# Query, key and value products of eight tiles in three wide steps, with scratch ordered by query, key and value

## The chip, the cores and the metric

The kernel runs on one core of a Trainium2 chip. The metric is device time in microseconds (us) for one execution. The core has five engines with an instruction stream each: PE (TensorE, matrix multiplication; its weight loads are listed apart as PEld), DVE (VectorE), ACT (ScalarE), POOL (GpSimd) and SP (SyncE, which here issues all DMA transfers).

## The reference

One transformer block on 2048 rows of 512 numbers: a normalisation without scale or shift, attention over a dilated local window, a residual, another normalisation, a squared-ReLU MLP and a second residual.

```python
S, D, H, Dh, W, dil, F = 2048, 512, 32, 16, 8, 2, 1792

def layernorm(x): return (x - mean(x)) / sqrt(var(x) + 1e-5)

def attention(x):
    q, k, v = split(x @ wqkv)              # each S x 512: 32 heads of 16
    # row s looks at rows s, s-2, s-4, ... s-14; rows below 0 are masked
    logits = q[s] . k[s - 2*w] * Dh**-0.5  # w = 0..7, per head
    o = softmax(logits over w) @ v[s - 2*w]
    return o @ wo

h   = x + attention(layernorm(x))
r   = maximum(layernorm(h) @ w1 + b1, 0)
out = h + (r * r) @ w2 + b2
```

## The kernel before

**Tiles and steps.** The 2048 rows are cut into 16 tiles of 128 rows, numbered t = 0 to 15. A tile is not 128 neighbouring rows: partition p of a tile holds every eighth row, `i = t % 4` and the parity `e` of the row being fixed in a tile, so that the rows of a window (two apart) lie in the same parity `e`. The attention and the MLP work in eight steps s = 0 to 7 of two tiles (`RI = 2`); four tiles (`R = 4`) with the same half of the rows and the same parity form a unit.

**Matrix products.** Every product is done in three passes of reduced-width operands: each factor is split in a high part (a cast, `hi`) and a low part (the difference, `lo`). `mm3` issues the twelve matmuls of one product over four blocks of the inner dimension: four of high by high, four of low activations by high weights, four of high activations by low weights. The casts run on ScalarE; the differences on VectorE or GpSimd.

**Slots.** The program order is written out by hand. `now["slot"]` counts slots, one product (or one MLP step) each. A product's neighbours are put down with `at(d, fn)`, to be issued d slots later, and `after(d, fn)`, the same but behind the slot's attention work. `end_slot(pe)` closes a slot: it adds the declared TensorE time `pe` to `now["pe"]`, issues what is due (`run(due)`), then lets `pump` take pieces from the generator `attention()` until the declared VectorE time `now["dve"]` has caught up with `now["pe"]`, then issues the `late` list. `transposes` and some other functions add to these two counters as well. The numbers are declared costs of this planner, not measurements; they only set the order of the instructions.

**Query, key and value (tiles 0 to 15).** For each tile: `load_x`, `x_stats` (statistics on VectorE, the reciprocal root on GpSimd), `x_norm` (ScalarE for t >= 4), `x_T` (four TensorE transposes, with a cast to `xh` on ScalarE and a difference `xl` on VectorE), then four products `qkv(t, gp)`. A product has 384 columns: 128 of the query, 128 of the key and 128 of the value, of two of the eight groups of heads. Its result lies in one of four PSUM banks in turn (`bank()`: `mm`, `mm`, `acc0`, `acc1`). One slot later `evac` copies it on ScalarE into a half of the staging buffer `y2`, beside the result of the other tile of the pair; when both are there, `store` sends this to the scratch `qkv_d` in DRAM, in one transfer. `store_halo` copies, for each of four `gp`, the pad rows that the first window needs, inside the scratch, two slots after the store of tile 0. `stored` notes which (unit, gp) the attention may read.

Slots 0 to 15 are the products of tiles 0 to 3. `first_phase(t0)` then does tiles t0 and t0 + 1 in eight slots, for t0 = 4, 6, 8, 10, 12 and 14 (slots 16 to 63), and prepares tiles t0 + 2 and t0 + 3 meanwhile: `x_stats` in its slots 0 and 1, `x_norm` in 4 and 5, `x_T` in 6 and 7. In its even slots `weight_job` loads a piece of `wo` or `w1` into `raw`; five slots later ScalarE casts it and GpSimd takes the difference. The phases of tiles 12 and 14 also contain the beginning of step 0 behind the attention: `o_T` (transposes of the attention's result `o`, cast to `oh` on ScalarE, difference `ol` on VectorE), `wo_product`, `h_add` (residual and statistics, VectorE), `h_norm` and `h_T`.

**Attention.** The generator `attention()` runs through 32 items (s, gp), each of which covers two tiles and two groups of heads: loads of `k`, `v`, `q` from the scratch, `dots` and its sums on VectorE, the exponential on ScalarE, and `weigh`, a product on VectorE followed by three halving additions on GpSimd, which end in `o`. The first eight items take gp in the outer loop; from step 2 on, all four gp of a step follow each other.

**MLP.** For each step, 14 slots: `mlp1(s, f)` makes 128 columns of the hidden layer (twelve matmuls of 256 columns), `hidden` one slot later activates, squares and casts it on ScalarE and takes the low part `rl` on GpSimd (VectorE in the last step), and `mlp2` adds the block to the output three slots later (`LAG`). Between them stand the next step's `o_T` (slots 3 and 4) and `wo_product` (slots 6 and 7). In the first MLP block the weights `w2` come in as well: `load_w2` into a `raw2`, and `split_w2`.

**Staging rows.** `row()` gives out buffers of 128 x 512 from one pool of `ROWS = 15`; `xt`, `xh`, `xl`, `raw`, `raw2`, `h`, `hn`, `oh`, `ol`, `hh` and `hl` all live there. When all are taken, the next writer waits for the last reader of the oldest. The last low part of `w2`, `w2_l[13]`, lives in a row as well, since the buffer of `y2`, reused for `w2` behind the products, has room for three blocks of 512.

Of the kernel before, what the change touches and what calls it, by code (L numbers as in the profile page):

```python
# [8 lines left out]
F32 = mybir.dt.float32  # L9
F32R = mybir.dt.float32r  # L10
# [4 lines left out]
S, D, H, DH, W, F = 2048, 512, 32, 16, 8, 1792  # L15
P = 128
KB = D // P
FB = F // P
R = 4
RI = 2  # L20
NS = S // P // RI
G = 8
GH = H // G
GC = GH * DH
CH = S // 2
PAD = W
EPS = 1e-5
NEG = -4.0e9
ROWS = 15
LAG = 3  # L30
SLOW = 1.1
DELAY = 3
# [6 lines left out]
def block_kernel(ctx, tc, x, wqkv, wo, w1, b1, w2, b2, out):  # L39
    nc = tc.nc  # L40

    const = ctx.enter_context(tc.tile_pool(name="const", bufs=1))
    wpool = ctx.enter_context(tc.tile_pool(name="wpool", bufs=1))
# [3 lines left out]
    dram = ctx.enter_context(tc.tile_pool(name="dram", bufs=1, space=bass.MemoryType.DRAM))  # L47
# [1 line left out]
    ctx.enter_context(tc.manual_schedule())  # L49

    CS = (CH + PAD) * GC
    qkv_d = dram.tile([2, G // 2, 3, 2, CH + PAD, GC], F32, name="qkv_d")

    def chain(e, g, c, r, ap):
        block = ((e * (G // 2) + g // 2) * 3 + c) * 2 + g % 2
        return bass.AP(tensor=qkv_d.tensor, offset=qkv_d.offset + block * CS + r * GC, ap=ap)


# [12 lines left out]
    wq_h = wpool.tile([P, KB, 3 * D], F32R, name="wq_h", tag="big_h")  # L73
    wq_l = wpool.tile([P, KB, 3 * D], F32R, name="wq_l", tag="big_l")
# [4 lines left out]
    w2_h, w2_l = {}, {}  # L79

    def row(name, shape=(P, D), dt=F32):
        return work.tile(list(shape), dt, name=name, tag="row", bufs=ROWS)

# [7 lines left out]
    def at(delta, fn, *a):  # L91
        due.setdefault(now["slot"] + delta, []).append((fn, a))

    def after(delta, fn, *a):
        late.setdefault(now["slot"] + delta, []).append((fn, a))

    def end_slot(pe):
        now["pe"] += pe
        run(due)
        pump()  # L100
        run(late)
        now["slot"] += 1

    def run(chores):
        todo = chores.get(now["slot"], [])
        while todo:
            fn, a = todo.pop(0)
            fn(*a)
# [43 lines left out]
    def transposes(src):  # L152
        tr = psum.tile([P, KB, P], F32, name="tr", bufs=2)
        for k in range(KB):
            nc.tensor.transpose(tr[:, k, :], src[:, k * P:(k + 1) * P], ident)  # L155
        now["pe"] += 0.45
        return tr
# [14 lines left out]
    def mm3(ps, lh, ll, rh, rl):  # L172

        terms = [(lh, rh, k) for k in range(KB)] + [(ll, rh, k) for k in range(KB)]
        terms += [(lh, rl, k) for k in range(KB)]
        for n, (l, r, k) in enumerate(terms):
            nc.tensor.matmul(ps, l(k), r(k), start=(n == 0), stop=(n == 3 * KB - 1))  # L177
# [4 lines left out]
    stored = set()  # L182
# [160 lines left out]
    def pump(until=None):  # L343

        while (done[until] < G) if until is not None else (now["dve"] < now["pe"]):
            t = next(stream, "end")
            if t == "end":
                now["dve"] = 1e9
                return
            if t is None:  # L350
                now["dve"] = max(now["dve"], now["pe"])
                return
            dve(t * SLOW)


    xt, xT = {}, {}
# [13 lines left out]
    def x_T(t):  # L370
        tr = transposes(xt.pop(t))
        xT[t] = row("xh", (P, KB, P), F32R), row("xl", (P, KB, P), F32R)
        at(0, hi_T, tr, [xT[t][0]])
        after(0, lo_T, tr, [xT[t][0]], [xT[t][1]])

    nbank = [0]

    def bank():
        tag = ("mm", "mm", "acc0", "acc1")[nbank[0] % 4]
        nbank[0] += 1  # L380
        return psum.tile([P, D], F32, name="mm", tag=tag, bufs=2 if tag == "mm" else 1)


    GP = 2 * GC

    def pair(w, k, gp):
        return w[:, k].rearrange("p (c n) -> p c n", c=3)[:, :, gp * GP:(gp + 1) * GP]
# [4 lines left out]
            nc.sync.dma_start(chain(0, g, 2, 0, [[G * 3 * CS, 2], [GC, PAD], [1, GC]]),  # L392
                              chain(0, g, 2, PAD, [[0, 2], [0, PAD], [1, GC]]))

    def store(t, gp, y):
        b, r = divmod(t, 8)
        e, i = divmod(r, 4)
        nc.sync.dma_start(chain(e, 2 * gp, 0, PAD + CH // 2 * b + i,
                                [[R * GC, P], [CS, 6], [1, RI * GC]]), y)
        if t == 0:  # L400
            at(2, store_halo, gp)
        if i == R - RI:
            stored.add((t // R, gp))

    ys = {}
    y2 = wpool.tile([P, 2, 6, RI * GC], F32, name="y2", tag="y2")

    def evac(t, gp, ps):
        if t % RI == 0:
            ys[gp] = y2[:, nbank[0] // RI % 2]  # L410
        y = ys[gp]
        nc.scalar.copy(y[:, :, t % RI * GC:(t % RI + 1) * GC],  # L412
                       ps[:, :3 * GP].rearrange("p (j c) -> p j c", j=6))
        if t % RI == RI - 1:
            at(0, store, t - t % RI, gp, ys.pop(gp))

    def qkv(t, gp):

        ps = bank()
        xh, xl = xT[t]  # L420
        mm3(ps[:, :3 * GP], lambda k: xh[:, k, :], lambda k: xl[:, k, :],
            lambda k: pair(wq_h, k, gp), lambda k: pair(wq_l, k, gp))
        at(1, evac, t, gp, ps)

    raws = {}

# [39 lines left out]
    def o_T(s, j):  # L466
        pump(until=s)
        tr = transposes(o_t[s][:, j, :])
        oT[s, j] = row("oh", (P, KB, P), F32R), row("ol", (P, KB, P), F32R)
        at(0, hi_T, tr, [oT[s, j][0]])  # L470
        after(0, lo_T, tr, [oT[s, j][0]], [oT[s, j][1]])
# [13 lines left out]
    def wo_product(s, j):  # L485
        ps = psum.tile([P, D], F32, name="wo", tag="tr", bufs=2)
        oh, ol = oT.pop((s, j))
        mm3(ps, lambda k: oh[:, k, :], lambda k: ol[:, k, :],
            lambda k: wo_h[:, k, :], lambda k: wo_l[:, k, :])
        at(1, h_add, s, j, ps)  # L490
        after(3, h_norm, s, j)
# [3 lines left out]
    def h_T(s, j):  # L495
        if j == 0:
            hT[s] = ([row("hh", (P, KB // 2, RI, P), F32R) for _ in range(2)],
                     [row("hl", (P, KB // 2, RI, P), F32R) for _ in range(2)])
        hh, hl = hT[s]
        tr = transposes(hn.pop((s, j)))  # L500
        hs_, ls_ = [t[:, :, j] for t in hh], [t[:, :, j] for t in hl]
        due.setdefault(now["slot"], []).insert(0, (hi_T, (tr, hs_)))
        at(0, lo_T, tr, hs_, ls_)
# [87 lines left out]
    for n in range(16):  # L591
        gp, t = divmod(n, 4)
        if n in (1, 2):
            x_T(n + 1)
        qkv(t, gp)
        if n < 6:
            for k in (0, 1):
                at(0, hi_wqkv, n // 2 + 1, n % 2 * 2 + k)
                after(0, lo_wqkv, n // 2 + 1, n % 2 * 2 + k,
                      nc.gpsimd if k else nc.vector)  # L600
        if n == 1:
            load_wqkv(3)
        if n == 13:
            consts()
        if n in (5, 6, 12, 14):
            at(0, load_x, n - 1 if n < 7 else n // 2)
        if n in (8, 9):
            at(0, x_stats, n - 4)
        if n in (12, 13):
            at(0, x_norm, n - 8)  # L610
        if n in (14, 15):
            x_T(n - 10)
        end_slot(1.95)
# [3 lines left out]
    def first_phase(t0):  # L617
        for n in range(8):
            gp, t = n // 2, t0 + n % 2
            if t0 + 3 < 16:  # L620
                if n in (0, 1):
                    at(0, x_stats, t0 + 2 + n)
                if n in (4, 5):
                    at(0, x_norm, t0 - 2 + n)
                if n in (6, 7):
                    x_T(t0 - 4 + n)
            if t0 + 5 < 16 and n in (4, 6):
                at(0, load_x, t0 + 2 + n // 2)
            k = 8 * ((t0 - 12) // 2) + n - 4
            if k in (10, 11):  # L630
                h_T(0, k - 10)
            qkv(t, gp)
            if jobs and n % WJ == 0:
                at(0, weight_job)
            if k in (0, 1):
                at(0, load_h, 0, k)
                o_T(0, k)
            if k in (3, 4):
                wo_product(0, k - 3)
                now["pe"] += 2.6  # L640
            if k in (7, 8, 9):
                at(0, load_w2, k - 7)
            end_slot(1.95)

    def load_w2(f):
        raws[f] = row("raw2")
        nc.sync.dma_start(raws[f], w2[f * P:(f + 1) * P, :])

    for t in range(R, 16, RI):
        first_phase(t)  # L650


    big2_h = wpool.tile([P, 12, D], F32R, name="w2_h", tag="big_h")
    big2_l = wpool.tile([P, 12, D], F32R, name="w2_l", tag="big_l")
    big2_x = wpool.tile([P, 3, D], F32R, name="w2_x", tag="y2")
    for f in range(12):
        w2_h[f], w2_l[f] = big2_h[:, f, :], big2_l[:, f, :]
    w2_h[12], w2_l[12], w2_h[13] = [big2_x[:, n, :] for n in range(3)]
    w2_l[13] = row("w2l", dt=F32R)

    def split_w2(f):
        raw = raws.pop(f)
# [63 lines left out]
```

## Time and profile before

| | us |
|---|---|
| three runs, timed | 535.2, 536.5, 537.06 (median 536.5) |
| the profiled execution, timed | 534.84 |
| its span, from first to last instruction | 533.1 |
| TensorE busy | 520.7 (98%), 3186 matmuls and transposes |
| VectorE busy | 376.1 (71%) |
| GpSimd busy | 317.9 (60%) |
| ScalarE busy | 262.1 (49%) |
| granted TensorE clock, mean | 1.0 |

How to read the lines that follow. A row of a timeline gives the start in the span, the time that the row covers, the engine, the source line, the operation, what it writes <- what it reads, the shapes, how many instructions the row holds, and in brackets the idle time of the engine before it with what released it. SPq is the queue of DMA issues on SP. Matmuls overlap in time, so that the price of one is the distance between two starts, not its duration. In a row of a wait the numbers are the total, the count and the longest. In a row of a stretch stand, after the length, the busy time of PE, PEld, DVE, ACT and POOL with the number of instructions, the granted clock, the share of the DMA engines' time and GB/s. A row of the chain of waits that ended last begins with the time in the span and the length. Line numbers are those of the kernel above.

### The profile page before, as it was taken

The page shows a single profiled execution, that of the slowest core. Times are in us where ns is not written, and L with a number is a line of the kernel's source. Part 1 is how long each engine was busy: PE and PEld are TensorE (multiplying, and loading weights), DVE is VectorE, ACT ScalarE, POOL GpSimd, SP SyncE. Part 2 cuts the span into 40 slices and gives each one's busy share as a digit, 9 for nine tenths or more (in the row PEclk, how much of TensorE's full clock was granted, in tenths as well). Part 3 has the DMA queues.
Part 4 walks back from the last instruction along what each step waited for, and adds up shares of the span by engine and source line. Part 5 has one row for each costly group of instructions (what it writes and reads, how often), then busy time and mean ns, then how long its engine had stood idle before and what let it go on. Part 6 is the DMA issues. An engine that isn't in the chain of part 4 may idle for free.

```text
span 533.1 us, 9022 instructions
## 1 busy us (share of the span) xinstructions
PE 520.7 (98%) x3186; PEld 479.1 (90%) x3186; DVE 376.1 (71%) x569; ACT 262.1 (49%) x607; POOL 317.9 (60%) x435
## 2 busy tenths in 40 slices
PE   6999999999999989999999999999999999999996
PEld 5899999999999868988989898898989889898995
DVE  5569999887897898996998699599869502202111
ACT  4524554455248446545636454563645445254541
POOL 4515499687495398778678677867867852251000
PEclk9999999999999999999999999999999999999999
DMA  8577979687587453633643364364434102001001
GB/s 251 155 233 196 298 234 317 201 269 239 159 252 263 135 157 91 191 116 102 182 142 108 111 190 119 100 183 137 112 106 140 44 0 81 1 0 41 2 0 41
DMA packets 70661, 75.96 MB, mean 143 GB/s; under 512 B 6744, under 2 KB 47704, under 8 KB 70616
## 3 DMA queue, kind: packets, MB, share of 16 engines
q1 hardware_dynamic: 70616, 75.39, 46.7%
q8 instruction: 25, 0.41, 0.3%
q14 instruction: 20, 0.16, 0.1%
HBM read 58.50 MB, written 16.91 MB: 141 GB/s over the span
## 4 chain that ended last, share of the span: by engine, by line
PE 61%; POOL 2%; DVE 0%; ACT 0%; issue 0%; POOLq 0%
PE mm L177 27%; PE acc L530 9%; PE acc L532 9%; PE acc L531 9%; PE wo L177 6%; PE tr L155 2%; POOL pr L292 1%; POOL rl L118 1%; POOL h L483 0%; POOL rs L134 0%; DVE pr L283 0%; POOL rs L132 0%; DVE h L537 0%; ACT hh L115 0%; POOL o L292 0%
## 5 line engine op out<-in xcount | busy, mean ns | idle before, releaser
L292 POOL TENSOR_TENSOR pr<-pr 128x512 f32<-128x512 f32 (+1 forms) x128 | 133.0, 1039 | 47.6 <-DVE pr L283 42.5
L118 POOL TENSOR_TENSOR rl<-r,rh 128x256 fp32r<-128x256 f32 x98 | 72.1, 739 | 82.9 <-ACT rh L115 73.6
L509 ACT ACTIVATE r<-mm,b_sb 128x256 f32<-128x256 f32 x112 | 53.3, 476 | 123.1 <-PE mm L177 112.3
L272 DVE TENSOR_TENSOR pr<-qp,k 128x1024 f32<-128x1024 f32 x64 | 76.0, 1187 | 5.8 <-ACT qp L216 3.5
L283 DVE TENSOR_TENSOR pr<-ex,v 128x1024 f32<-128x1024 f32 x64 | 77.9, 1217 | 2.8
L532 PE MATMUL acc<-w_h,rl 128*128 128x512 f32 x192 | 75.0, 391 | 2.7 <-POOL rl L118 2.7
L530 PE MATMUL acc<-w_h,rh 128*128 128x512 f32 x192 | 76.5, 398 | 0.0
L531 PE MATMUL acc<-w_l,rh 128*128 128x512 f32 x192 | 75.9, 395 | 0.0
L177 PE MATMUL mm<-hh,w_h 128*128 128x256 f32 x448 | 72.5, 284 | 0.0
L177 PEld LDWEIGHTS mm<-hh,w_h 128*128 128x128 f32 x448 | 66.4, 189 | 6.5
L177 PE MATMUL mm<-hl,w_h 128*128 128x256 f32 x448 | 72.0, 283 | 0.0
L177 PE MATMUL mm<-hh,w_l 128*128 128x256 f32 x448 | 72.0, 283 | 0.0
L177 PEld LDWEIGHTS mm<-hl,w_h 128*128 128x128 f32 x448 | 61.8, 192 | 0.0
L177 PEld LDWEIGHTS mm<-hh,w_l 128*128 128x128 f32 x448 | 61.7, 192 | 0.0
L412 ACT COPY y<-mm 128x384 f32<-128x384 f32 x64 | 30.1, 480 | 63.6 <-PE mm L177 40.0
L177 PE MATMUL mm<-wq_h,xh 128*128 128x384 f32 x256 | 56.7, 342 | 0.3 <-ACT wq_h L115 0.3
L177 PE MATMUL mm<-wq_l,xh 128*128 128x384 f32 x256 | 55.3, 335 | 0.2 <-DVE wq_l L118 0.2
L177 PE MATMUL mm<-wq_h,xl 128*128 128x384 f32 x256 | 55.0, 335 | 0.4 <-DVE xl L118 0.4
L118 DVE TENSOR_TENSOR hl<-tr,hh 128x256 fp32r<-128x256 f32 x32 | 12.1, 418 | 56.8 <-ACT hh L115 56.8
L510 ACT ACTIVATE r<-r 128x256 f32<-128x256 f32 x112 | 46.9, 418 | 3.5
L115 ACT CAST rh<-r 128x256 fp32r<-128x256 f32 x112 | 45.6, 407 | 3.6
L532 PEld LDWEIGHTS acc<-w_h,rl 128*128 128x128 f32 x192 | 36.1, 188 | 11.8 <-POOL rl L118 3.6
(78 smaller groups left out, 869.3 us busy)
## 6 DMA issues: line engine op xcount, KB each, us to landing
k<-qkv_d SPq DMA_DIRECT2D x48, 288.0 KB, 2.8
v<-qkv_d SPq DMA_DIRECT2D x48, 288.0 KB, 2.7
qkv_d<-y SPq DMA_DIRECT2D x32, 384.0 KB, 3.9
xt<-in_A_x_dram SPq DMA_DIRECT2D x16, 256.0 KB, 4.2
q<-qkv_d SPq DMA_DIRECT2D x32, 128.0 KB, 2.8
h<-in_A_x_dram SPq DMA_DIRECT2D x16, 256.0 KB, 4.0
out_dram<-h SPq DMA_DIRECT2D x16, 256.0 KB, 3.2
raw<-in_B_w_dram SPq DMA_DIRECT2D x16, 224.0 KB, 4.3
```

Source lines behind the costliest of these rows:

```text
L115: nc.scalar.copy(dst, src)
L118: eng.tensor_tensor(out=dst, in0=src, in1=h, op=ALU.subtract)
L177: nc.tensor.matmul(ps, l(k), r(k), start=(n == 0), stop=(n == 3 * KB - 1))
L272: nc.vector.tensor_tensor(out=pr.rearrange("p i w h d -> p i w (h d)"), in0=qp[:, j].unsqueeze(2).to_broadcast([P, RI, W, GC]), in1=kwin, ...
L283: nc.vector.tensor_tensor(out=p2, in1=vwin, op=ALU.mult, in0=e1[:, :, :, j * GH:(j + 1) * GH].unsqueeze(4).to_broadcast([P, RI, W, GH, DH]))
L292: nc.gpsimd.tensor_tensor(out=dst, in0=p2[:, :, :w], in1=p2[:, :, w:2 * w], op=ALU.add)
L412: nc.scalar.copy(y[:, :, t % RI * GC:(t % RI + 1) * GC], ps[:, :3 * GP].rearrange("p (j c) -> p j c", j=6))
L509: nc.scalar.activation(r, ps, AF.Relu, bias=b1_sb[:, f:f + 1])
L510: nc.scalar.activation(r, r, AF.Square)
L530: nc.tensor.matmul(a, rh[:, js], w2_h[f], start=(f == 0), stop=False)
L531: nc.tensor.matmul(a, rh[:, js], w2_l[f], start=False, stop=False)
L532: nc.tensor.matmul(a, rl[:, js], w2_h[f], start=False, stop=(f == FB - 1))
```

## The change

- Tiles 4 to 11 go through a new `middle_phase(t0)`: six slots for a pair of tiles instead of eight. A slot is one product `qkv_of(t, c)` of 512 columns: all of the query (c = 0), the key (1) or the value (2) of one tile. Tiles 0 to 3 and 12 to 15 keep their products of 384 columns.
- In a middle phase the next pair's `x_stats` stand in slots 0 and 1, `x_norm` in 3 and 4, `x_T` in 4 and 5, `load_x` in 3 and 5, and the weight jobs in 0, 1, 3 and 4. A slot declares 2.65.
- The scratch is ordered by parity, then query/key/value, then the eight groups of heads; before, the pair of groups came ahead of query/key/value. A wide product's result is stored in one transfer of 512 KB for a pair of tiles; a narrow product's result (384 KB) now takes two transfers, one for each group. For tiles 4 to 11 a unit is noted in `stored` only behind the value's store, for all four `gp` at once.
- A half of `y2` grows from six to eight blocks of 64 columns. Its buffer then has room for four blocks of `w2`, so `w2_l[13]` moves there from a row of the pool, and the pool has 14 rows.

```diff
-ROWS = 15
+ROWS = 14
...
-    qkv_d = dram.tile([2, G // 2, 3, 2, CH + PAD, GC], F32, name="qkv_d")
+    qkv_d = dram.tile([2, 3, G, CH + PAD, GC], F32, name="qkv_d")
 
     def chain(e, g, c, r, ap):
-        block = ((e * (G // 2) + g // 2) * 3 + c) * 2 + g % 2
+        block = (e * 3 + c) * G + g
...
-    def store(t, gp, y):
+    def store(t, gp, c, y):
         b, r = divmod(t, 8)
         e, i = divmod(r, 4)
-        nc.sync.dma_start(chain(e, 2 * gp, 0, PAD + CH // 2 * b + i,
-                                [[R * GC, P], [CS, 6], [1, RI * GC]]), y)
+        pos = PAD + CH // 2 * b + i
+        if c is None:
+            for j in range(2):
+                nc.sync.dma_start(chain(e, 2 * gp + j, 0, pos,
+                                        [[R * GC, P], [G * CS, 3], [1, RI * GC]]), y[:, :, j])
+        else:
+            nc.sync.dma_start(chain(e, 0, c, pos, [[R * GC, P], [CS, G], [1, RI * GC]]), y)
         if t == 0:
             at(2, store_halo, gp)
         if i == R - RI:
-            stored.add((t // R, gp))
+            if c is None:
+                stored.add((t // R, gp))
+            elif c == 2:
+                stored.update((t // R, gp) for gp in range(G // 2))
 
     ys = {}
-    y2 = wpool.tile([P, 2, 6, RI * GC], F32, name="y2", tag="y2")
-
-    def evac(t, gp, ps):
+    y2 = wpool.tile([P, 2, G, RI * GC], F32, name="y2", tag="y2")
+
+    def evac(t, gp, c, ps):
+        j = 6 if c is None else G
         if t % RI == 0:
-            ys[gp] = y2[:, nbank[0] // RI % 2]
-        y = ys[gp]
+            ys[gp, c] = y2[:, nbank[0] // RI % 2, :j]
+        y = ys[gp, c]
         nc.scalar.copy(y[:, :, t % RI * GC:(t % RI + 1) * GC],
-                       ps[:, :3 * GP].rearrange("p (j c) -> p j c", j=6))
+                       ps[:, :j * GC].rearrange("p (j c) -> p j c", j=j))
         if t % RI == RI - 1:
-            at(0, store, t - t % RI, gp, ys.pop(gp))
+            if c is None:
+                y = y.rearrange("p (c j) n -> p c j n", c=3)
+            at(0, store, t - t % RI, gp, c, y)
+            del ys[gp, c]
+
+    def qkv_of(t, c):
+
+        ps = bank()
+        xh, xl = xT[t]
+        cs = slice(c * D, (c + 1) * D)
+        mm3(ps, lambda k: xh[:, k, :], lambda k: xl[:, k, :],
+            lambda k: wq_h[:, k, cs], lambda k: wq_l[:, k, cs])
+        at(1, evac, t, 0, c, ps)
...
-        at(1, evac, t, gp, ps)
+        at(1, evac, t, gp, None, ps)
...
+    def middle_phase(t0):
+        for n in range(6):
+            c, t = n // 2, t0 + n % 2
+            if n in (0, 1):
+                at(0, x_stats, t0 + 2 + n)
+            if n in (3, 4):
+                at(0, x_norm, t0 - 1 + n)
+            if n in (4, 5):
+                x_T(t0 - 2 + n)
+            if n in (3, 5):
+                at(0, load_x, t0 + 4 + n // 4)
+            qkv_of(t, c)
+            if n % 3 != 2:
+                at(0, weight_job)
+            end_slot(2.65)
...
     for t in range(R, 16, RI):
-        first_phase(t)
+        middle_phase(t) if t < 12 else first_phase(t)
...
-    big2_x = wpool.tile([P, 3, D], F32R, name="w2_x", tag="y2")
+    big2_x = wpool.tile([P, 4, D], F32R, name="w2_x", tag="y2")
     for f in range(12):
         w2_h[f], w2_l[f] = big2_h[:, f, :], big2_l[:, f, :]
-    w2_h[12], w2_l[12], w2_h[13] = [big2_x[:, n, :] for n in range(3)]
-    w2_l[13] = row("w2l", dt=F32R)
+    w2_h[12], w2_l[12], w2_h[13], w2_l[13] = [big2_x[:, n, :] for n in range(4)]
```

## Prediction

> **What bounds the kernel now.** I read the page first, then the table of waits, then busy time by stretch, and last the timelines of the engines around the two places that the change touches.
>
> ```profile
> span 533.1 us, 9022 instructions
> PE 520.7 (98%) x3186; PEld 479.1 (90%) x3186; DVE 376.1 (71%) x569; ACT 262.1 (49%) x607; POOL 317.9 (60%) x435
> ```
>
> ```profile
> PEclk9999999999999999999999999999999999999999
> ```
>
> ```profile
> PE acc L532 <- POOL rl L118: 2.7, 2, 2.0
> ```
>
> ```profile
> 47.00:117.50 70.50, 70.50 (x419) 69.99 (x418) 65.84 (x97) 34.89 (x76) 53.09 (x73) 1.00 0.84 258
> ...
> 159.10:209.30 50.20, 47.40 (x293) 41.72 (x293) 42.34 (x64) 30.68 (x72) 33.72 (x42) 1.00 0.51 161
> ```
>
> The columns after the length are PE, PEld, DVE, ACT, POOL, the granted clock, the DMA share and GB/s. TensorE is the bound: in the stretch of tiles 4 to 11 (47.0 to 117.5) it never idles, and its clock is full. So whatever is saved in the matmul stream there comes off the end, and whatever makes TensorE wait there is added. The first MLP block (159.1 to 209.3) has the one hole behind it: 50.2 us of which 47.4 are busy, and two waits for GpSimd's `rl` make up 2.7 of the idle time. VectorE is at 93% in the stretch that is changed (65.84 of 70.50), and ScalarE, though half idle, carries the copies out of PSUM, the norms and the casts in one fixed order.
>
> **The products.** Start-to-start intervals are the price of a matmul here, since the durations overlap.
>
> ```profile
> 38.57 0.85 PE L177 MATMUL mm<-wq_h,xl 128*128 128x384 f32 x4
> ...
> 40.65 0.85 PE L177 MATMUL mm<-wq_h,xl 128*128 128x384 f32 x4
> ```
>
> ```profile
> 135.96 1.09 PE L177 MATMUL wo<-wo_h,oh 128*128 128x512 f32 x4
> 136.88 1.09 PE L177 MATMUL wo<-wo_h,ol 128*128 128x512 f32 x4
> ```
>
> ```profile
> 269.83 2.72 PE wo L177 x12
> ```
>
> Twelve matmuls of 384 columns take 40.65 - 38.57 = 2.08 us, 173.3 ns each. Twelve of 512 take 2.72 us in the chain, 226.7 ns each. A tile now costs 4 x 2.08 = 8.32 us and will cost 3 x 2.72 = 8.16: the columns are the same 1536, and 12 of 48 matmuls go, with the part of each that isn't columns (173.3 and 226.7 lie on a line of 0.417 ns a column plus 13.3 ns). Eight tiles: 8 x 0.16 = **-1.28 us**, all on the path, since nothing waits there. The other end is the pair of rows at 135.96: in that mixed stretch four matmuls of 512 took 0.92 us, 230 ns each; at 36 x 230 = 8.28 us a tile the gain is 8 x 0.04 = 0.3 us. The slow ones stand right behind narrower products; the middle phases are 512 columns throughout, so I take the chain's value, with 0.04 off (12 x 3.4 ns) at each end of the stretch, where widths change: **-1.2**.
>
> The Trainium skill (TensorE: Matmul & The Clock Gate, Back-to-back issue gap) gives an isolated warm interval of N/2.4 + 2.5 ns. By that the change would bring only 96 x 2.5 ns = 0.24 us; the trace's 173.3 and 226.7 speak against the 2.5.
>
> **The norm that moves closer to its transpose.** Before, `x_norm` runs two slots ahead of `x_T` (n = 4, 5 and 6, 7), two products of 2.08 us. After, it is one slot ahead (n = 3, 4 and 4, 5), one product of 2.72. For most tiles that is enough:
>
> ```profile
> 90.76 0.85 PE L177 MATMUL mm<-wq_h,xh 128*128 128x384 f32 x4
> ```
>
> ```profile
> 91.01 0.48 ACT L412 COPY y<-mm 128x384 f32<-128x384 f32 x1 [1.61 <-PE mm L177]
> 91.39 0.82 ACT L150 ACTIVATE xt<-xt,rs 128x512 f32<-128x512 f32 x1
> ```
>
> The norm of tile 10 ends at 92.21, 1.45 us after a product began at 90.76, and a wide product leaves 2.72. For tile 6 it isn't enough, because there ScalarE is held up.
>
> ```profile
> 47.00 0.95 PE L177 MATMUL mm<-wq_h,xh 128*128 128x384 f32 x4
> ```
>
> ```profile
> 59.81 0.60 PE L155 MATMUL tr<-ident,xt 128*128 128x128 f32 x4
> ```
>
> ```profile
> 52.42 0.86 ACT L412 COPY y<-mm 128x384 f32<-128x384 f32 x2 [3.52 <-DMA qkv_d<-y]
> 57.97 0.86 ACT L412 COPY y<-mm 128x384 f32<-128x384 f32 x2 [4.69 <-PE mm L177]
> 58.71 0.83 ACT L150 ACTIVATE xt<-xt,rs 128x512 f32<-128x512 f32 x1
> ```
>
> ```profile
> 47.91 0.38 SPq L398 DMA_DIRECT2D qkv_d<-y  x1
> 48.34 0.54 SPq L209 DMA_DIRECT2D q<-qkv_d  x1
> 52.34 1.19 SPq L392 DMA_DIRECT2D qkv_d<-qkv_d  x2
> 53.62 0.35 SPq L450 DMA_DIRECT2D raw<-in_A_wo_dram  x1
> 54.07 0.38 SPq L398 DMA_DIRECT2D qkv_d<-y  x1
> ```
>
> ```profile
> DMA to landing us min/median/max: 2.6/3.9/6.5
> ```
>
> Products 16, 17, 18 start at 47.00, 49.1, 51.2 (2.08 apart), so the copy of product 18 could begin about 53.5; yet ScalarE begins it at 57.97 (the row puts the wait down to TensorE, which was long done). It needs the half of `y2` that the store issued at 54.07 reads, and 54.07 + 3.9 is 57.97. That store was late because SP stood from 48.9 to 52.34 before the halo copies, which need the store of 47.91 landed (47.91 + 0.38 + 3.9 = 52.2). Behind the two copies the norm of tile 6 ends at 59.54, and TensorE comes to its transpose at 59.81: 0.27 us to spare.
>
> After, TensorE arrives at that transpose behind four wide products: 47.00 + 4 x 2.72 = 57.88. The norm now stands behind the copy of product 18 alone. With the same landing: 57.97, one copy of 512 columns (0.5, as the next instruction starts 0.48 behind the 512-wide `oh` cast quoted below), the norm 0.83, and 0.2 that I allow to TensorE: 59.5, so TensorE waits 1.6 us. On top come the stores of tiles 0 to 3, issued in two pieces: one issue of 0.38 us more for each, and one to four of these delays arrive here, +0.4 to +1.5. Against that, a piece of half the size may land at the fastest 2.6 instead of 3.9, -1.3. So the wait lies between 0.3 and 3.1; I take **+2.1**, nearer the middle of the row's own landing time than its minimum. What hides this afterwards: nothing, as TensorE has no slack before 190. Tile 7 follows with the same copies already done, and tiles 8 to 11 I price at nothing, by the rows of tile 10.
>
> The Trainium skill (Perfetto Trace Analysis, DMA Optimizations) says that splitting transfers may let the whole end sooner if the DMA engines are mostly idle; the share is 0.84 here, so I don't count on it.
>
> Behind the waiting store on SP stand the next loads of k, v, q, x and the weights, and for those VectorE waits; TensorE waits for no attention before the output products, so half a microsecond there costs nothing. The stores of tiles 4 to 11 become 12 of 512 KB instead of 16 of 384, with three slots of 2.72 between uses of a buffer half instead of three of 2.08: relief, worth nothing at the end. The copies, 6 wide for 8 narrow, hide on ScalarE (34.89 busy of 70.50). That tiles 4 to 7 are all stored only behind their third product costs nothing: by the planner's own clock their last store goes out near 67, and the first item that reads them begins at 103.
>
> **One staging row less.** In program order 15 rows are live or asked for at two places. When the second transposed output of step 0 is cast (slot 5 of the phase of tile 12): 2 `h`, 2 + 2 `oh`/`ol`, 4 `xh`/`xl`, 2 `xt`, 3 `raw`. With 14, `ol` waits for GpSimd to finish with a `raw`.
>
> ```profile
> 131.78 0.69 DVE L118 TENSOR_TENSOR ol<-tr,oh 128x512 fp32r<-128x512 f32 x1 [0.56 <-issue]
> ```
>
> ```profile
> 139.29 0.68 DVE L118 TENSOR_TENSOR xl<-tr,xh 128x512 fp32r<-128x512 f32 x1
> ```
>
> ```profile
> 143.59 0.87 PE L177 MATMUL mm<-wq_h,xh 128*128 128x384 f32 x4
> ```
>
> ```profile
> 133.91 1.16 POOL L118 TENSOR_TENSOR w_l<-raw,w_h 128x448 fp32r<-128x448 f32 x1
> ```
>
> VectorE would stand from 131.8 to 135.1. Behind it `xl` of tile 15 moves from 139.97 to 143.3; TensorE asks for it behind four matmuls of the product at 143.59, at 144.3. 1 us is left: price 0, up to 1 if that cover is gone.
>
> The second place is slot 4 of the first MLP block: 4 `h`, 4 `hh`/`hl`, 2 `oh`/`ol`, 4 `raw2` are 14, and two more are asked for. The trace shows what the 16th does:
>
> ```profile
> 174.82 0.69 DVE L118 TENSOR_TENSOR ol<-tr,oh 128x512 fp32r<-128x512 f32 x1 [3.78 <-PE wo L177]
> ```
>
> ```profile
> 173.64 1.07 PE L177 MATMUL wo<-wo_h,ol 128*128 128x512 f32 x4
> ...
> 175.45 0.64 PE L177 MATMUL mm<-hh,w_h 128*128 128x256 f32 x4
> ```
>
> ```profile
> 170.00 0.59 ACT L115 CAST oh<-tr 128x512 fp32r<-128x512 f32 x1 [1.51 <-DVE w_l L118]
> 170.48 0.62 ACT L115 CAST w_h<-raw 128x512 fp32r<-128x512 f32 x1
> 171.00 0.48 ACT L509 ACTIVATE r<-mm,b_sb 128x256 f32<-128x256 f32 x1
> ```
>
> It waits 3.78 us for the output product that frees a row. With 14, `oh` waits for the same product as well; `oh` is ScalarE's, which has `hidden` of block 4 behind it, and the next product but one needs that PSUM bank. The four readings of `ol` start at 173.64, 0.227 apart, so the last has ended near 174.8. From `oh` to the end of that activation ScalarE takes 1.48 us in the rows (170.00 to 171.48), so the bank is free at 176.3 to 176.4, while TensorE wants it at 175.45: **+0.9**, from 0 (the free row comes from elsewhere) to 2.
>
> **The planner.** A pair of tiles declares 6 x 2.65 + 0.9 = 16.8 instead of 8 x 1.95 + 0.9 = 16.5, so four pairs declare 1.2 more. Adding the declared costs slot by slot, the same attention work (139.31) is out when the MLP begins, against 139.3 now and 138.1 before; from there each `weigh` falls one slot earlier: item 10's second from slot 5 to 4, item 11's from 7 and 9 to 6 and 8.
>
> ```profile
> 186.76 2.44 POOL L292 TENSOR_TENSOR pr<-pr 128x512 f32<-128x512 f32 x2 [4.82 <-DVE pr L283]
> ```
>
> GpSimd idled 4.82 us before this group of item 11, and was late with the `rl` behind it. Weighing one slot earlier puts the group ahead of `h_add`, its statistics and a weight's low part on VectorE, which the planner declares at 0.62 + 0.93 + 0.62 us, and takes away the shorter of the two waits, 2.7 - 2.0; but the two following groups, 2.44 us each and a last addition, now stand ahead of an `rl` that they stood behind. I take **-0.6** of the 2.7, between -2.7 and +3.
>
> **Sum:** -1.2 + 2.1 + 0.9 - 0.6 = +1.2 us. The profiled execution took 534.84 us (span 533.1), 1.66 under the median of 536.5; it becomes 536.0, and the median 537.7. A measurement of this kernel tells about 0.3%, 1.6 us, from no change, so this lies within it, on the slow side.
>
> **The rivals.** *The waits don't come* (0.25): the half stores land near the 2.6 us, tile 6 costs 0.3, and GpSimd, started sooner, loses its 2.7 us of lateness. -1.2 + 0.3 - 2.0 + 0.5 = -2.4: 534.1. For it: 4.82 us of idle GpSimd to fill. Against it: the landing of 3.9 that fits both rows.
>
> *GpSimd's new order* (0.2), the slow side: in the first MLP block two groups of 2.44 us and a little pass ahead of an `rl` that TensorE needs within three slots. It decides if VectorE delivers item 11's second weighing later than two slots (5.6 us) after its place; then each group is waited for nearly in full and 2.7 becomes some 5.2. Without my -0.6 the sum is +1.8, and 2.5 more make +4.3 at worst; at half of that delay it is about +3: 539.5. For it: VectorE is busy for 42.34 of 50.20 us in this stretch, most of its idle time lies before the group (3.78 at 174.82). Against: the group before it leaves earlier.
>
> *The wide products run at 230 ns* (0.05): gain 0.3 instead of 1.2, +2.1: 538.6. By the 2.5 ns of the Trainium skill (TensorE: Matmul & The Clock Gate, Back-to-back issue gap) the time would come out near there too.
>
> That the products stay as many can't be: the counts are in the code.
>
> **The numbers.** The forecast has 0.5: 0.3 of it within 1.6 us, 0.2 above, as its bounds run from about -1 to +3. Faster: 0.22 from the first rival. Same: 0.3 + 0.03 + 0.02 = 0.35. Slower: 0.2 + 0.2 + 0.03 = 0.43. The range goes from the first rival, 534.0, to near the worst of the second, 540.5; the forecast's own is 535.5 to 539.5.
>
> **What would show it.** 36 matmuls a tile 227 ns apart; the transpose of tile 6 waiting 1 to 3 us for ScalarE's norm, with a copy of `y` before it that waits for a store; `oh` of the first MLP block on ScalarE waiting for the output product; an idle of TensorE near 1 us behind that product, and 2 us for `rl`. A gapless stretch of tiles 4 to 11 would prove me wrong by 2 us, and no wait for `rl` by as much again.

## The result, and the profile after

The changed kernel takes 538.35 us (median of 8 runs, 538.0 to 539.0), the kernel before 536.38 (8 runs, 534.8 to 537.06): 1.0047 times as long, with a 95% interval of 1.0035 to 1.0059, so slower by 0.5%. The page of the changed kernel begins:

```profile
span 536.3 us, 8832 instructions
PE 521.2 (97%) x3090; PEld 467.3 (87%) x3090; DVE 382.4 (71%) x569; ACT 261.4 (49%) x599; POOL 317.1 (59%) x435
```

The 96 matmuls are gone and the span is 3.2 us longer. Its table of waits, of TensorE (total, times, longest), says why:

```profile
PE mm L176 <- ACT r L530: 2.0, 2, 1.0
PE acc L553 <- POOL rl L117: 1.6, 2, 0.9
PE wo L176 <- DVE xl L117: 1.6, 1, 1.6
PE tr L154 <- ACT xt L149: 1.3, 1, 1.3
```

Before, the one such entry behind the start was `rl` with 2.7. Three of these four are new. The stretches of tiles 4 to 11 and of the first MLP block, which the prediction showed of before (length, then busy PE, PEld, DVE, ACT, POOL, the granted clock, DMA share, GB/s):

```profile
46.90:117.20 70.30, 69.00 (x321) 56.82 (x319) 66.52 (x98) 33.96 (x67) 51.95 (x73) 1.00 0.85 252
161.10:212.70 51.60, 47.95 (x293) 41.57 (x293) 46.89 (x67) 30.80 (x72) 34.09 (x42) 1.00 0.49 154
```

TensorE now idles 1.3 us in the first, and 3.65 in the second for 2.8 before. To see where the time goes, the program is cut at instructions that every kernel has, and the distance between their starts on TensorE is taken from the traces (us; "wide" kernels have the change's products). From MLP block 1 to TensorE's last matmul all of them take 319.6.

| kernel | `x_T`(5) to first `o_T` | to first output product | to MLP block 0 | to its block 7 | to MLP block 1 |
|---|---|---|---|---|---|
| before | 81.29 | 8.02 | 23.13 | 21.90 | 28.35 |
| before, second profile | 82.59 | 8.02 | 23.13 | 21.90 | 28.35 |
| before, 14 rows | 82.03 | 8.58 | 23.22 | 22.84 | 29.56 |
| before, halo later | 81.06 | 8.04 | 23.13 | 21.91 | 28.42 |
| changed (wide, 14 rows) | 81.56 | 9.82 | 23.19 | 23.13 | 28.50 |
| wide, 14 rows, 2.6 declared | 81.17 | 8.83 | 23.23 | 22.83 | 28.38 |
| wide, 15 rows | 81.48 | 8.36 | 23.26 | 21.91 | 28.25 |
| wide, 15 rows, 2.6 declared | 81.77 | 8.02 | 23.13 | 21.91 | 29.59 |
| wide, 15 rows, halo later | 80.04 | 8.36 | 23.23 | 21.90 | 28.26 |

The first column holds the products and the transpose of tile 6. In the rows with the halo later, where nothing waits, it goes from 81.06 to 80.04: the wide products save 1.02 us. The changed kernel gives back three times that, 1.80 in the second column and 1.23 in the fourth.

**Tile 6, changed kernel** (timelines of ScalarE and TensorE):

```profile
57.99 0.58 ACT L421 COPY y<-mm 128x512 f32<-128x512 f32 x1 [4.38 <-DMA qkv_d<-y]
58.47 0.81 ACT L149 ACTIVATE xt<-xt,rs 128x512 f32<-128x512 f32 x1
59.34 0.65 PE L154 MATMUL tr<-ident,xt 128*128 128x128 f32 x4 [1.30 <-ACT xt L149]
```

The copy starts where the prediction put it, 57.97, now named as waiting for the store, and the transpose stands behind it.

**Ahead of the first output product, changed kernel** (ScalarE, GpSimd, VectorE, TensorE):

```profile
135.04 0.59 ACT L114 CAST xh<-tr 128x512 fp32r<-128x512 f32 x1 [2.76 <-POOL w_l L117]
133.85 1.16 POOL L117 TENSOR_TENSOR w_l<-raw,w_h 128x448 fp32r<-128x448 f32 x1
137.18 0.68 DVE L117 TENSOR_TENSOR xl<-tr,xh 128x512 fp32r<-128x512 f32 x1
137.91 1.18 PE L176 MATMUL wo<-wo_h,oh 128*128 128x512 f32 x4 [1.64 <-DVE xl L117]
```

ScalarE stands until GpSimd's low part frees a row at 135.0; the cast of tile 14 is late, so is its low part on VectorE, and TensorE doesn't begin the output product, because `wo` and the transposes share two PSUM buffers (the tag `tr`) and the one it wants still holds what `xl` reads.

**First MLP block, changed kernel** (ScalarE, then TensorE):

```profile
176.77 0.59 ACT L114 CAST oh<-tr 128x512 fp32r<-128x512 f32 x1 [6.84 <-PE wo L176]
...
178.07 0.48 ACT L530 ACTIVATE r<-mm,b_sb 128x256 f32<-128x256 f32 x1
...
178.60 0.73 PE L176 MATMUL mm<-hh,w_h 128*128 128x256 f32 x4 [0.97 <-ACT r L530]
```

`oh` stands until an output product gives a row back, the activation `r` stands behind it on ScalarE, and TensorE waits for the PSUM bank that `r` reads.

### The profile page after: what moved, and what is told of

The parts are those of the page before. It is cut to its first block, busy times and chain, and to the rows that moved or that the text cites. A ratio compares the mean times of both kernels' runs of the same rounds, so it can differ in the third digit from the quotient of the medians.

```text
span 536.3 us, 8832 instructions
## 1 busy us (share of the span) xinstructions
PE 521.2 (97%) x3090; PEld 467.3 (87%) x3090; DVE 382.4 (71%) x569; ACT 261.4 (49%) x599; POOL 317.1 (59%) x435
## 4 chain that ended last, share of the span: by engine, by line
PE 60%; POOL 3%; DVE 2%; issue 1%; POOLq 0%; DVEq 0%
PE mm L176 26%; PE acc L551 9%; PE acc L552 9%; PE acc L553 8%; PE wo L176 6%; PE tr L154 2%; POOL pr L291 1%; POOL rl L117 1%; DVE pr L282 0%; POOL h L504 0%; DVE st L125 0%; DVE w_l L117 0%; DVE h L496 0%; DVE lg L319 0%; DVE h L558 0%
## 5 line engine op out<-in xcount | busy, mean ns | idle before, releaser
L421 ACT COPY y<-mm 128x384 f32<-128x384 f32 (+1 forms) x56 | 29.2, 526 | 57.0 <-PE mm L176 33.6
L176 PE MATMUL mm<-wq_h,xh 128*128 128x384 f32 (+1 forms) x224 | 55.6, 370 | 0.0
L176 PE MATMUL mm<-wq_h,xl 128*128 128x384 f32 (+1 forms) x224 | 53.9, 362 | 0.4 <-DVE xl L117 0.4
L176 PE MATMUL mm<-wq_l,xh 128*128 128x384 f32 (+1 forms) x224 | 53.4, 360 | 0.0
L176 PEld LDWEIGHTS mm<-wq_h,xl 128*128 128x128 f32 x224 | 41.3, 190 | 4.7 <-DVE xl L117 0.8
```

Of the source, the lines that this page charges most:

```text
L421: nc.scalar.copy(y[:, :, t % RI * GC:(t % RI + 1) * GC], ps[:, :j * GC].rearrange("p (j c) -> p j c", j=j))
```

## The experiments

Each was run beside the kernel before, in three rounds on three chips; ratios are to the kernel before on the same chip.

### The kernel before, once more

> The kernel before, unchanged, once more: its profile of 534.84 us lies 1.5 under its median of 536.38, so what do its other executions spend? Theory of waits: products and transposes take the same time in every execution, and the spread of 534.8 to 537.06 lies in TensorE's few waits; a longer span than 533.1 shows a longer wait for the transpose of tile 6 (0.27 us to spare before) or for rl in the first MLP block (3.3 us of excess in the first profile, start to start). Rival: the spread is even, each stage a little longer. Time 536.4, within 0.2% of the runs beside it.

536.03 us, ratio 0.9997 (0.9986 to 1.0007). Its profile has 536.12 us, span 534.3, and the 1.2 us more than in the first profile lie in one stage, the first column. Timelines of ScalarE and TensorE in this second profile:

```profile
59.42 0.86 ACT L412 COPY y<-mm 128x384 f32<-128x384 f32 x2 [4.65 <-DMA qkv_d<-y]
60.17 0.82 ACT L150 ACTIVATE xt<-xt,rs 128x512 f32<-128x512 f32 x1
61.05 0.66 PE L155 MATMUL tr<-ident,xt 128*128 128x128 f32 x4 [0.69 <-ACT xt L150]
```

TensorE waits for the norm of tile 6 in the kernel before as well; some 0.4 us more lie at tile 5's `xl`, 50.37. The 0.27 us to spare were those of one execution. What differs is a landing: the store of `y` ahead of the halo copies is issued at 47.91 and 47.89, but SP's wait for it is 3.4 us in the first profile and 4.9 in the second (waits of SP's queue):

```profile
SPq L392 <- DMA qkv_d<-y: 3.4, 1, 3.4
```

```profile
SPq L392 <- DMA qkv_d<-y: 4.9, 1, 4.9
```

### The norm two slots ahead again

> The changed kernel with x_norm of the middle phases one slot earlier (slots 2 and 3, two slots ahead of the transpose as before the change). Theory of waits: the norm of tile 6 then stands ahead of the copy of product 18, TensorE no longer stands 1.35 us at its transpose, and all that follows comes 1.35 us earlier: 537.0. Rival, attention sets the pace: GpSimd's w_l that frees the row at 135.0 depends on VectorE and not on TensorE, so the wait ahead of the first output product grows from 1.8 to 3.1 us and the time stays 538.3.

```diff
-            if n in (3, 4):
-                at(0, x_norm, t0 - 1 + n)
+            if n in (2, 3):
+                at(0, x_norm, t0 + n)
```

538.06 us, ratio 1.0037 (1.0025 to 1.005): 0.3 less than the changed kernel, not 1.35. The wait at tile 6 is gone, and the wait ahead of the output product has not grown, so the rival is wrong as it stood. But its thought came true elsewhere: VectorE, busy 66.52 us of the 70.30 of that stretch in the changed kernel, gives tile 9's `xl` too late for a TensorE that comes earlier (TensorE, this run):

```profile
86.42 1.20 PE L176 MATMUL mm<-wq_h,xl 128*128 128x512 f32 x4 [0.49 <-DVE xl L117]
```

In this profile that takes back 0.65 us start to start, and its first tiles were 0.56 later than the changed kernel's.

### Fifteen rows; and both

> The changed kernel with 15 staging rows again (2 KB won by one buffer instead of two for q and for lg, and by placing zero in an unused part of y2). Theory of waits: ScalarE's xh of tile 14 no longer waits 2.76 us for GpSimd's w_l, and its oh of the first MLP block no longer 6.84 us for the output product; TensorE's waits of 1.8 us ahead of the first output product and of 1.2 us ahead of block 5 of the first MLP block go: 538.35 - 3.0 = 535.3. The wait of 1.35 us at tile 6 stays. Rival, attention sets the pace: TensorE comes 3.0 us earlier to the second half of the first MLP block and waits there so much longer for rl and for ScalarE (3.3 us now, 6 then): 538.

> Both edits together: 15 rows and x_norm two slots ahead. Theory of waits: the terms add, 538.35 - 1.35 - 3.0 = 534.0; what is left against the kernel before is the 1.05 us that the wide products save and the stores in two pieces, so 0.4% faster than before. Rival, attention sets the pace: no faster than the better of the two alone, 535.3 to 537.

```diff
-ROWS = 14
+ROWS = 15
...
-    zero = const.tile([PAD, GC], F32, name="zero")
+    zero = y2[:PAD, 1, 6, :GC]            # behind the allocation of y2
...
-        q = att.tile([P, 2, RI, GC], F32, name="q")
+        q = att.tile([P, 2, RI, GC], F32, name="q", bufs=1)
...
-                lg = att.tile([P, RI, W, 2, GH], F32, name="lg")
+                lg = att.tile([P, RI, W, 2, GH], F32, name="lg", bufs=1)
```

15 rows: 535.1 us (expected 535.3), ratio 0.9977 (0.9967 to 0.9988), faster than the kernel before. In ScalarE's timeline the cast of tile 14 no longer stands, and the fourth column is back at 21.91:

```profile
132.20 0.61 ACT L113 CAST xh<-tr 128x512 fp32r<-128x512 f32 x1
```

The one row costs the changed kernel 538.35 - 535.1 = 3.2 us, 2.7 of them in the two columns (9.82 - 8.36 and 23.13 - 21.91). (The edit makes single buffers of `q` and `lg` as well, so 3.2 is the row less whatever that costs, which no run shows apart.) With the norm early as well: 534.8, ratio 0.9975 (0.9965 to 0.9986). The expected 534.0 was missed: between these two the timed runs show no difference, though the profiles do (533.6 and 532.6 of span). What the early norm is worth is a few tenths here, and I can't say it closer.

### Fourteen rows in the kernel before

> The row part alone in the kernel before: 14 rows, y2 with eight blocks of which the narrow products use six, w2_l[13] in it; products, stores and scratch as before. Theory of rows: the two waits that 14 rows made in the changed kernel need nothing else of the change, so TensorE stands about 1.8 us ahead of the first output product and 1.2 us in the first MLP block: 536.3 + 3.0 = 539.3. Rival, the waits come only where the new order of the attention's pieces puts GpSimd's w_l late: 536.3 to 537.5.

```diff
-ROWS = 15
+ROWS = 14
...
-    y2 = wpool.tile([P, 2, 6, RI * GC], F32, name="y2", tag="y2")
+    y2 = wpool.tile([P, 2, G, RI * GC], F32, name="y2", tag="y2")
```

(`evac` takes the first six blocks; `w2_l[13]` in `y2` as in the change.) 537.27 us against 536.01, ratio 1.003 (1.0017 to 1.0043): +1.3 by the medians and 1.6 by the ratio, half of what was expected. The time is in the rival's range, yet both waits are there without the rest of the change, 0.56 (8.58) and 0.94 (22.84) in place of 1.8 and 1.2: so the rows alone don't explain 3.2.

### The scratch and the stores alone

> The order of the scratch alone in the kernel before, and with it stores in two pieces for all 16 tiles (64 transfers for 32); 15 rows, 384 columns throughout. Theory: the path doesn't see it but at the transpose of tile 6, where the kernel before already waits 0 to 1.3 us in its two profiles, and where the later stores add up to 1: 536.3 to 537.3. Rival, SP's queue: 32 more issues of 0.4 to 0.5 us each hold up the loads for the attention, and so GpSimd and the first MLP block: 538 or more.

```diff
-    qkv_d = dram.tile([2, G // 2, 3, 2, CH + PAD, GC], F32, name="qkv_d")
+    qkv_d = dram.tile([2, 3, G, CH + PAD, GC], F32, name="qkv_d")
...
-        block = ((e * (G // 2) + g // 2) * 3 + c) * 2 + g % 2
+        block = (e * 3 + c) * G + g
...
-        nc.sync.dma_start(chain(e, 2 * gp, 0, PAD + CH // 2 * b + i,
-                                [[R * GC, P], [CS, 6], [1, RI * GC]]), y)
+        y = y.rearrange("p (c j) n -> p c j n", c=3)
+        for j in range(2):
+            nc.sync.dma_start(chain(e, 2 * gp + j, 0, PAD + CH // 2 * b + i,
+                                    [[R * GC, P], [G * CS, 3], [1, RI * GC]]), y[:, :, j])
```

535.5 us against 536.01, ratio 0.9994 (0.9982 to 1.0006): less than the theory's 536.3, and no cost that can be told, although 32 transfers are issued more. More issues on SP's queue as a cost of the change are out; SP standing before the halo copies is another matter, below.

### What a wide slot declares

> The changed kernel with 15 rows and 2.6 declared for a wide slot instead of 2.65, so that a pair of tiles declares 16.5 as before the change and the attention's pieces fall in the first MLP block as they did before. Theory: the shift was worth nothing (block 7 of the first MLP block to the next block's start took 28.36 us before the change and 28.26 with 15 rows): 535.1 within 0.5, with the waits of 0.92 and 2.15 us for rl of the kernel before in place of 1.07, 0.86 and 1.1. Rival, the step of the prediction: the later order was worth 0.6, so 535.7 or more.

> The changed kernel (14 rows) with 2.6 declared for a wide slot, so that the attention's pieces lie as before the change. 14 rows cost 3.2 us in the changed kernel (538.35 against 535.1) but 1.3 in the kernel before (537.27 against 536.0). Theory of order: the difference comes from where the declared 16.8 puts the attention's pieces around tile 14's cast, so with 2.6 the wait ahead of the first output product falls from 1.6 to about 0.5 us, and the cost of 14 rows against the same kernel with 15 (535.77) is 1.3 to 1.6: 537.2. Rival, the wide products themselves make the rows scarce: 3.2 us again, 539.0.

```diff
-            end_slot(2.65)
+            end_slot(2.6)
```

With 15 rows: 535.77 us, ratio 0.9993 (0.9981 to 1.0006), 0.7 more than with 2.65, though the two intervals overlap a little. With 14: 537.56, ratio 1.003 (1.0016 to 1.0044). So with 2.6 the lost row costs 1.8 us, with 2.65 3.2, and the wait ahead of the output product falls from 1.80 to 0.81: the later order of the attention's pieces makes the same missing row dearer. It costs 0.34 there without any row missing (8.36 against 8.02), and in return the timed runs with 15 rows give it 0.7. The profiles' 28.25 against 29.59 overstate this: with 2.6 the slowest of twelve executions was profiled, one in which the granted clock fell.

The clock of each execution is on record. A fall to half for 3.4 us, as the last section shows it, lowers the mean of 534 us by 0.003; the mean tells that a whole fall came, not where. Medians (and numbers) of the executions at 0.997 or less, and of those above:

| kernel | 0.997 or less | above |
|---|---|---|
| before, in the three rounds | 536.48 to 536.54 (61) | 535.27 to 535.54 (32) |
| wide, 15 rows, 2.6 declared | 536.26 (7) | 534.86 (5) |
| wide, 15 rows | 535.53 (1) | 534.96 (11) |
| wide, 14 rows, 2.6 declared | 538.34 (7) | 536.28 (5) |

Where the clock didn't fall, the two declared costs give the same time with 15 rows, 534.86 and 534.96. So by these executions the order of 2.65 shortens nothing by itself; its 0.7 is that the clock falls in one execution of twelve instead of seven. The lost row costs 1.4 there with 2.6 (536.28 - 534.86), and is still dearer with 2.65.

### The addition of b2 moved

> The changed kernel with 15 rows, x_norm two slots ahead, and GpSimd's addition of b2 to h moved 12 slots on (out of the first MLP block, where two of them of 1.75 and 1.29 us stand between rl's). Theory: the waits for rl near the end of that block (0.86 and 1.1 us) go, 534.8 - 2.0 = 532.8; the wait of 1.07 us for ScalarE's activation behind the exponential stays. Rival, GpSimd is late there by the attention's additions, which wait for VectorE, and the moved additions make other rl late: 534.8.

```diff
-        nc.gpsimd.tensor_tensor(out=h, in0=h, in1=b2_sb, op=ALU.add)
+        after(12, lambda: nc.gpsimd.tensor_tensor(out=h, in0=h, in1=b2_sb, op=ALU.add))
```

534.93 us, ratio 0.9984 (0.9975 to 0.9993): no gain over 534.8. I had overlooked step 0: its two additions, 12 slots on, now fall into the same block (GpSimd, 185.84 and 187.82). The waits for `rl` are gone, but ScalarE, whose activation stands behind the exponential in its order, makes TensorE wait instead (ScalarE, then TensorE):

```profile
193.46 0.28 ACT L337 ACTIVATE ex<-lg 128x128 f32<-128x128 f32 x1 [3.67 <-DVE lg L333]
...
194.88 1.01 PE L175 MATMUL mm<-hh,w_h 128*128 128x256 f32 x4 [2.05 <-ACT r L530]
```

### The halo copies later

> The changed kernel with 15 rows, and the halo copies of the last three pairs of groups issued five slots behind the store of tile 0 instead of two; x_norm stays one slot ahead. Theory: the norm of tile 6 is late because SP stands before the halo copies until a store has landed, and the next stores queue behind; with the halo later SP goes on, the copies of y come earlier and the wait at the transpose of tile 6 (1.06 us of excess in the run with 15 rows) goes: 535.1 - 1.0 = 534.1. Rival, the stores land late by themselves, halo or not: 535.1, wait as before.

> 15 rows, x_norm two slots ahead, and the halo copies later. Theory: with the norm early the wait of tile 6 is gone already (534.8), so the halo adds nothing on the path: 534.8. Rival, a freer ScalarE and SP also bring the attention's loads earlier and shorten the waits in the first MLP block (3.3 us): 533.5.

> The kernel before with the halo copies later, nothing else. Theory: its executions spread over 534.4 to 537.8 because the transpose of tile 6 waits 0 to 1.3 us for the same stall of SP; without it the median falls by about 0.8 to 535.4 and the upper end below 537. Rival, the spread comes from the first MLP block, where the granted clock falls to 0.6 for 3 us in some profiles behind the wait of 2.4 us for rl (1.2 us more): median 536.2 and the same spread.

```diff
-            at(2, store_halo, gp)
+            at(2 if gp == 0 else 5, store_halo, gp)
```

Wide products, 15 rows, halo later: 534.1 us as expected (five executions), ratio 0.9964 (0.9951 to 0.9977), the lowest median here; the interval overlaps that of 15 rows alone. SP goes on, the stores behind follow, and the norm ends 1 us before TensorE comes (SP's queue, ScalarE, TensorE):

```profile
48.28 1.20 SPq L390 DMA_DIRECT2D qkv_d<-qkv_d  x2
...
50.99 0.90 SPq L400 DMA_DIRECT2D qkv_d<-y  x2
```

```profile
55.39 0.59 ACT L421 COPY y<-mm 128x512 f32<-128x512 f32 x1 [1.43 <-DMA qkv_d<-y]
55.87 0.82 ACT L148 ACTIVATE xt<-xt,rs 128x512 f32<-128x512 f32 x1
...
57.67 0.60 PE L153 MATMUL tr<-ident,xt 128*128 128x128 f32 x4
```

In the changed kernel the same two pieces went out at 54.15. So in this profile the norm one slot ahead is near enough, and SP's stall is the cause at tile 6. With the norm early besides: 534.38, ratio 0.9969 (0.9957 to 0.9981), nothing more, and the first MLP block is no shorter. In the kernel before, the edit gives 535.27, ratio 0.9991 (0.9979 to 1.0002): the direction is the expected one and the profile has no wait there, but the timed difference isn't clear of none, and its runs spread from 534.5 to 536.46, those of the kernel before beside it from 534.79 to 537.71. Where the clock didn't fall, the two take the same, 535.22 (six executions) and 535.27 (eight): for the spread the rival, the clock, is the likelier account.

## Why the prediction was right or wrong

The forecast was 537.7 and slightly slower; 538.35 came. The total is near by luck: two terms are wrong in opposite directions, and a third came out near its size by a mechanism that the prediction didn't have.

- **Products**, -1.2: right in kind, 1.02 in size. A product behind a product takes 2.72 us as predicted; one behind a transpose takes 2.85, and there is one for each tile, not two for the whole stretch as I had put the 0.04. The narrow products had the same: 2.17 behind a transpose, 2.08 else. So a tile goes from 8.41 to 8.29, and eight tiles save 1.0. The kernel before, then the changed one:

```profile
62.71 0.94 PE L177 MATMUL mm<-wq_h,xh 128*128 128x384 f32 x4
...
64.88 0.85 PE L177 MATMUL mm<-wq_h,xh 128*128 128x384 f32 x4
...
66.96 0.85 PE L177 MATMUL mm<-wq_h,xh 128*128 128x384 f32 x4
```

```profile
80.24 1.18 PE L176 MATMUL mm<-wq_h,xh 128*128 128x512 f32 x4
...
83.09 1.07 PE L176 MATMUL mm<-wq_h,xh 128*128 128x512 f32 x4
...
85.81 0.39 PE L176 MATMUL mm<-wq_h,xh 128*128 128x512 f32 x1
```

- **Tile 6**, +2.1: the mechanism is as told, store, copy, norm and transpose, and the wait in the changed kernel is 1.3, for the 1.6 of the working; the 0.5 added for stores in two pieces is not seen, the store went out at 54.15 as before at 54.07. The step that failed is taking the 0.27 us to spare from one execution and adding the 1.66 us up to the median as if spread evenly: the second profile shows this same wait inside those 1.66, and part of them is the clock: in one round the kernel before has a median of 536.34, but 535.54 over the executions without a fall. In the first column the changed kernel lies 81.56 - 80.04 = 1.52 us above its time without waits, the kernel before 0.23 and 1.53 (81.29 and 82.59 less 81.06): the change's share is 0 to 1.3, depending on the execution.
- **The row, step 0**, priced at 0: wrong by 1.8. The place and the releaser were right, GpSimd's `raw` at 135.0. I had put the wait on VectorE's `ol`; it fell on the next to ask, ScalarE's `xh` of tile 14. And I looked for who needs the late `xl` among the readers of its row only. The output product needs the PSUM buffer from which that `xl` is made, and before the change it began at 135.96, 3.5 us ahead of the first matmul that reads tile 14's `xl`. 0.34 of it is the order, the rest the row.
- **The row, first MLP block**, +0.9: right, 1.23, by `oh`, the output product and the PSUM bank.
- **The planner**, -0.6: the waits changed places more than length, 2.7 for `rl` before, 1.6 for `rl` and 1.04 for ScalarE after (28.35 and 28.50). Against 2.6 declared, the timed runs with 15 rows give it 0.7, near the 0.6, but not by shorter waits: it is the clock, which I hadn't thought of. Where it doesn't fall the order is worth nothing.

Of the rivals, "the waits don't come" didn't happen in the changed kernel; that the kernel with 15 rows and the halo later measures its 534.1 is by another sum. "GpSimd's new order" didn't happen. The products at 230 ns did, as the mean of a tile (8.29 us for 36), but the gain wasn't that rival's 0.3, since the narrow ones were dearer than 8.32 too.

## What to carry to other kernels

When a pool shrinks by one, follow the instruction that will wait to every resource it holds up, the PSUM buffer that it reads as well as the tile that it writes; that was 1.8 us. A slack read from one execution is one sample: where a margin of 0.3 us decides a term, look at a second profile before putting a price on losing it, and compare medians only after a look at the granted clock of each execution. And when a change brings a saving with a cost attached, separate them: the wide products were worth their 1.0 us once the 2 KB for the row were found elsewhere.

## What the runs showed of the hardware

A wait can cost more than its length. Eight of the profiles have a TensorE idle of 2.0 us in the first MLP block (2.4 start to start). In four of them the granted clock fell to half for 3.41 us, beginning 0.3 to 1.5 us behind the idle, and the stage took up to 1.2 us longer (28.35 to 28.42 without, 29.56 to 29.61 with it in the kernels of that order). The same stretch in the kernel with the new scratch alone, and in the kernel before (PE, PEld, DVE, ACT, POOL busy, then the granted clock):

```profile
201.60:204.80 3.20, 3.20 (x15) 3.05 (x14) 2.30 (x3) 2.68 (x6) 3.20 (x4) 0.54 0.20 71
```

```profile
201.60:204.80 3.20, 3.20 (x22) 2.85 (x22) 2.73 (x3) 2.41 (x6) 3.12 (x4) 1.00 0.08 29
```

In the six profiles in which the same waiting was split into pieces of about 1 us, the clock stayed whole there. The Trainium skill (TensorE: Matmul & The Clock Gate, HAM oscillation — how this bites in real kernels) gives idle gaps above about 3.4 us as what throttles; here 2.0 us were enough in four of eight.

What parts the four from the four can be worked out from the traces' own records of the clock. In each profile all changes of the clock lie whole multiples of 3.413 us apart; with the new scratch alone they are at 10.69, 201.83, 205.25 and 532.93, which is 56, 1 and 96 such intervals apart. Laying this grid over the 2.0 us of idle time gives the longest piece of it in one interval:

| profile | longest piece, us | clock fell at the end of that interval |
|---|---|---|
| 15 rows, norm early, b2 moved | 2.05 | yes |
| before, new scratch alone | 2.01 | yes |
| wide, 15 rows, 2.6 declared | 2.01 | yes |
| before, 14 rows | 1.97 | yes |
| wide, 14 rows, 2.6 declared | 1.79 | no |
| before | 1.32 | no |
| before, second profile | 1.30 | no |
| before, halo later | 1.28 | no |

Over all 14 profiles the clock fell behind each of the 19 intervals in which TensorE's rows leave 1.97 us or more idle (the end of the program among them), and behind none of the 2137 with 1.63 or less; of two between, it fell behind the one of 1.73 (in the changed kernel, at 8.09 us) and not behind the one of 1.79. So in these traces a wait of 2.0 us is dear when it lies in one interval and not when a boundary cuts it, which differs from one execution to the next. No run moved a wait on purpose to show this.
